# Sliding-window attention and a tanh layer on one core: which transposes go by DMA, which pairs stay uncast, and another list of steps

## The chip, the core and the metric

The kernel runs on one core of a Trainium2 chip. TensorE (PE) multiplies matrices and also transposes by a product with the identity; VectorE (DVE), ScalarE (ACT) and GpSimd (POOL) work on elements; SyncE (SP) only issues transfers here. POOL issues transfers too, those that change float32 to bfloat16 on the way. Each engine runs its own instructions in order and waits for others at semaphores. The metric is the device time of one execution in microseconds (us). The median of 3 runs of the kernel before is 319.51 us (318.67 to 321.03).

## The reference, cut to what matters

```python
batch, n_heads, seq, head_dim = (8, 8, 576, 64)          # q, k, v in float32
n_tokens, d_model, d_ff = (4608, 512, 2048)

def _attn_ref(q, k, v):
    scores = scale * np.matmul(q, k.transpose(0, 1, 3, 2))
    rel = pos[:, None] - pos[None, :]
    mask = (rel >= 0) & (rel < 64)
    scores = np.where(mask, scores, -1000000000.0)
    attn = softmax(scores)                               # exp, divided by its sum
    return np.matmul(attn, v)

def _moe_ref(x, w_in, w_out):
    h = x @ w_in
    g = h - np.tanh(h)
    return g @ w_out
```

x is the attention's result with the heads side by side: 4608 rows (8 batches of 576 positions) of 512. Each position sees itself and the 63 before it.

## The kernel before

**Tiling.** The eight heads of a batch are handled as four pairs (head r and head r + 4), so there are 32 pairs, pair g being of batch g // 4. The 576 positions are nine windows of 64; a window's queries meet 128 keys, its own 64 and the 64 before. The two layers behind the attention take the 4608 rows in nine chunks of 512 rows, eight windows each: chunk 2 holds windows 16 to 23, so six of its windows are batch 2's (18 to 26), and three of chunk 3's.

**Staging.** PE needs q, k and x with the feature on the partitions. Three ways lead there. (1) A pair's rows of q or k are loaded (words `lq`, `lk`), cast or laid side by side (`cq`, `ck`), transposed by PE in six products of 96 rows (`Ep` for q, `Fp` for k, line 261) and evicted from PSUM by ACT or DVE (`Ea`, `Eb`, `Ec`, `Fc`). A pair that is not cast is transposed straight from its loaded rows in 12 smaller products (line 257). (2) For k of batches 3 to 7, 128 positions at a time are loaded by POOL (`lr`) and transposed by DMA, issued on SP (`tk`, line 181). (3) For q of later batches a whole batch is loaded (`LQ`), spread by POOL into zeroed rows (`z`, then `cz`, line 128), written to device memory from SP (`bo`, line 133) and read back transposed, from SP again (`td`, line 138). In the kernel before, batches 6 and 7 take way 3. x is transposed either by PE (`Xp`, line 453) with evictions (`Xc`) or by DMA from SP (`Y`, line 472); in the kernel before batches 3 to 7 go by `Y`.

**The rest of a pair.** `Rp` makes the scores (lines 289, 294, 300), `Rx` the exponentials on ACT (line 305), `M` masks them on DVE, `LV`, `lv`, `lt` load V, `Z`, `za`, `zb` copy V's rows so that each window finds its 128 keys together (lines 166, 167). `P` and `PP` multiply by V (lines 405, 418), `D`, `DR`, `DN` divide by the sum (DVE). Batch 0's pairs mask by a product with `hide` ahead of the scores; the mask for the others, `seen`, is made by `n` and put into PSUM by `N`.

**The two layers.** For each chunk, 16 words `H` (four products each, line 489) make the first layer, `A` its tanh on ACT (line 497), `G` the difference on DVE (line 503); 16 words `W` (four products each, line 522) make the second layer and `O` evicts (ACT or DVE) and stores it from SP. w_in comes in three loads `wi`, w_out in four `wo`, on POOL.

**Order.** Nothing reorders at run time. A string PLAN holds one word per step, in the order in which the steps are issued; `play` goes through it. A word such as `Rp.12.0.4` is the scores of pair 12, group 0, in PSUM bank 4; a last letter names the engine (p POOL, a ACT, v DVE, s SP). Since each engine keeps its own order, a word's place says only what it stands behind on its own engine. `U` is a filler product on PE that nothing needs.

Of the kernel before, what the change touches and what calls it, by code (L numbers as in the profile page):

```python
# [9 lines left out]
ALU = mybir.AluOpType  # L10
# [5 lines left out]
def kernel(  # L16
# [21 lines left out]
    M = d_ff // 128  # L38
# [197 lines left out]

    def make_mask():
        nc.gpsimd.memset(seen, 1.0)
        nc.gpsimd.affine_select(seen, seen, compare_op=ALU.is_ge, fill=0.0,
                                base=-1, pattern=[[1, 128]], channel_multiplier=-1)  # L240
        nc.gpsimd.affine_select(seen, seen, compare_op=ALU.is_ge, fill=0.0,
                                base=64, pattern=[[-1, 128]], channel_multiplier=1)
# [241 lines left out]

    def hp_mm(c, m, s):
        n = columns(s)
        hp = ps[:, m % 2 if c > 1 or s is not None else m % 3, n]
        for ki in range(4):
            nc.tensor.matmul(hp, w_in_tile(ki, m),  # L489
                             chunk_tile(c)[:, n.start // 64:n.stop // 64, ki % 2, 64 * (ki // 2):64 * (ki // 2) + 64],  # L490
                             start=(ki == 0), stop=(ki == 3))
        return hp
# [70 lines left out]
    def subtract():  # L563
# [4 lines left out]
        i=make_ident, u=make_warm, mv=pads_v, mt=pads_k, mq=pads_q, mk=pads_kw, U=warm_up, h=make_hide, n=make_mask, N=put_mask,  # L568
# [15 lines left out]
        H=first_layer, A=tanh, G=subtract, W=lambda: yp_mm(*step("W")), O=lambda e: y_out(*step("O"), e))  # L584

    def play(script):
# [5 lines left out]
        lk.0.s lq.0.s u U.11 mq.0 mt.1 mv.0 lk.3.p i lk.1.p mt.0 cq.0.a ck.0.a Fp.0.2 Fc.0.2.a ck.1.a U.3  # L592
        Fp.1.2 lq.1.p cq.1.a mq.1 Ep.0.3 Ec.0.3.a Fc.1.2.v LV.0.3 LV.0.1 LV.0.4 LV.0.2 U.4 Ep.1.3 Ec.1.3.a h
        U.4 Rp.1.1.4 Rx.1.1.4 LV.0.0 Rp.1.0.0 lq.3.p lk.2.p Fp.3.2 Rx.1.0.0 Rp.0.1.4 Fc.3.2.a Rx.0.1.4
        Rp.0.0.0 mv.1 Z.0 lq.2.p U.2 Ep.3.3 Ec.3.3.a Rx.0.0.0 U.1 Fp.2.2 Rp.3.1.4 Ep.2.3 lk.4.p lk.5.p
        lk.7.p lq.5.p wi.0 lq.4.p n lq.7.p P.0 ck.5.v Fc.2.2.a Rx.3.1.4 Ec.2.3.a D.0 Rp.3.0.0 Fp.5.3
        Fc.5.3.v cq.5.v Rp.2.1.4 P.1 ck.4.a Rx.3.0.0 Ep.5.3 D.1 Rp.2.0.0 Ea.5.3.a Rx.2.1.4 Rx.2.0.0 wi.1
        lk.6.p wi.2 lq.6.p lv.1.0.1 lv.1.1.0 lv.1.0.0 lt.1 lv.1.1.1 P.3 Eb.5.3.v Rp.5.0.4 D.3 Fp.4.3
        Xp.0.0.1.2 Rx.5.0.4 Fc.4.3.a Xc.0.0.1.2.a P.2 Xp.0.0.0.3 N Rp.5.1.4 Xc.0.0.0.3.a Rx.5.1.4 D.2
        Xp.0.1.0.3 ck.7.v cq.4.v Xc.0.1.0.3.v Xp.0.1.1.2 Rp.5.2.4 Ep.4.3 Xc.0.1.1.2.a H H H Rx.5.2.4  # L600
        Ea.4.3.a A Eb.4.3.a A G A G G ck.6.v cq.7.v Rp.4.2.4 Fp.7.3 Rx.4.2.4 Fc.7.3.a H A Rp.4.0.4 Rx.4.0.4
        G H A G H Fp.6.3 A Rp.4.1.4 H H G Fc.6.3.a A A Rx.4.1.4 Ep.7.3 H M.5 G G A Ea.7.3.a cq.6.v G H H A A
        H A Eb.7.3.v Rp.7.2.4 Ep.6.3 Ea.6.3.a Rx.7.2.4 lq.8.p wo.0 lk.8.p lq.9.p wo.1 wo.2 zb.1.0.p za.1.1.p
        zb.1.1.p wo.3 lk.9.p lv.1.3.1 lv.1.3.0 lv.1.2.1 lv.1.2.0 G G G H H H A cq.8.v za.1.0.v G M.4
        Eb.6.3.a Rp.6.0.4 H Ep.8.3 A A Rx.6.0.4 A Rp.7.0.4 PP.4 Rx.7.0.4 Rp.6.2.4 G G G ck.8.v DR.4 DN.4.1
        DN.4.0 DN.4.2 Rx.6.2.4 cq.9.v W Rp.6.1.4 Ea.8.3.a Eb.8.3.a Rx.6.1.4 W W W Fp.8.3 Fc.8.3.v Rp.7.1.4 W
        Ep.9.3 Ea.9.3.v Rx.7.1.4 ck.9.v W W W O.a W Eb.9.3.a Fp.9.3 Rp.8.2.4 O.a M.6 lk.10.p lk.11.p
        lr.3.2.1 mk lr.3.2.0 lq.11.p W Fc.9.3.a Rx.8.2.4 Xp.1.0.0.3 W Rp.9.2.4 M.7 za.1.3.v zb.1.3.p
        zb.1.2.v za.1.2.v PP.6 DR.6 DN.6.2 DN.6.0 lq.10.p DN.6.1 Rx.9.2.4 Xc.1.0.0.3.a Rp.9.1.4 W Rx.9.1.4
        Xp.1.0.1.3 Xc.1.0.1.3.a Rp.8.0.4 W ck.10.v Rx.8.0.4 W Xp.1.1.1.3 Xc.1.1.1.3.a Rp.8.1.4 W LV.2.4  # L610
        LV.2.0 lr.3.0.0 LV.2.3 LV.2.2 lr.3.3.0 cq.10.v LV.2.1 lr.3.4.1 lr.3.0.1 lr.3.3.1 tk.3.3 tk.3.0
        tk.3.2 LQ.3 lr.3.1.1 lr.3.4.0 lr.3.1.0 Xp.1.1.0.3 W Rx.8.1.4 ck.11.v cq.11.v Xc.1.1.0.3.v Ep.10.3
        Ea.10.3.v Rp.9.0.4 tk.3.4 lr.4.2.0 tk.3.1 LQ.4 lr.4.3.0 LV.3.4 lr.4.1.0 lr.4.2.1 LV.3.3 lr.4.0.1
        lr.4.4.0 lr.4.0.0 lr.4.3.1 lr.5.0.1 tk.4.0 O.a O.a Eb.10.3.a H H A A H A Fp.10.3 M.8 G G H H G
        Rx.9.0.4 Fc.10.3.a A A Fp.11.3 Rp.10.1.4 H M.9 G G Fc.11.3.a Rx.10.1.4 A H A Rp.10.2.4 H Rx.10.2.4 A
# [74 lines left out]
```

## Time and profile before

| | |
|---|---|
| median of 3 runs | 319.51 us |
| the profiled execution's own time | 319.47 us |
| its span, from the first to the last instruction | 317.8 us |
| busy: PE, DVE, ACT, POOL | 305.3, 187.8, 173.2, 111.7 us |
| first-layer products (576) and second-layer products (560), mean of one | 379, 379 ns |
| first first-layer product | at 28.37 us |
| moved by DMA | 39.11 MB |
| fillers on PE | 25, 10.1 us busy |

A profile page shows the share of the span in which each engine was busy, the span in 40 slices with a digit of busy tenths each, the chain of work that ended last, and groups of instructions with their idle time and what released them. The timeline lists instructions by start and length. The weight loads of PE run beside its products, and a product's length overlaps the next one's. Idle time of an engine matters only where it sits on the chain.

### The profile page before, as it was taken

The numbers are of one execution on the slowest core, as the hardware profiler recorded it, in microseconds if no ns is written. First come the engines' busy times: TensorE is split into PE (matmuls) and PEld (weight loads), VectorE is DVE, ScalarE is ACT, GpSimd is POOL, SyncE is SP. The second block draws the span as 40 slices with busy tenths as digits, with TensorE's granted clock in tenths as the row PEclk, the third lists the DMA queues.
The fourth block names the chain that finished last, engine by engine and source line by source line (L and its number), as shares of the span: only waits on it lengthen the run. The fifth ranks groups of instructions, "written<-read, shape, count | busy, mean of one in ns | idle before, by whom it ended". The sixth has DMA issues, their size and how long they took to land.

```text
span 317.8 us, 6105 instructions
## 1 busy us (share of the span) xinstructions
PE 305.3 (96%) x2412; PEld 165.7 (52%) x2412; DVE 187.8 (59%) x321; ACT 173.2 (54%) x322; POOL 111.7 (35%) x164
## 2 busy tenths in 40 slices
PE   7878999999999999999799999999999999999995
PEld 2455565656655655555455555555554544445444
DVE  2355995489887896769374666566753554244400
ACT  4678885589778675555344635544524435334311
POOL 8982849985871384892021430000000000000000
PEclk9799999999999999999999999999999999999999
DMA  9999999999999699999998999262014010010021
GB/s 151 152 202 198 190 196 130 181 154 146 155 138 166 99 138 151 188 148 119 199 156 157 136 166 206 72 144 72 33 36 107 33 68 33 33 36 33 33 99 68
DMA packets 113133, 39.11 MB, mean 123 GB/s; under 512 B 96336, under 2 KB 107600, under 8 KB 113104
## 3 DMA queue, kind: packets, MB, share of 16 engines
q0 software_dynamic: 72064, 18.06, 66.4%
q1 hardware_dynamic: 41040, 20.65, 31.4%
q8 instruction: 19, 0.31, 0.4%
q14 instruction: 10, 0.08, 0.1%
HBM read 36.70 MB, written 11.80 MB: 153 GB/s over the span
## 4 chain that ended last, share of the span: by engine, by line
PE 86%; DMA 5%; DVE 4%; ACT 3%; issue 1%; SPq 0%; ACTq 0%; DVEq 0%
PE ps L489 37%; PE ps L522 36%; PE ps L300 4%; DMA xT<-xs 3%; PE ps L261 3%; PE ps L418 3%; PE ps L225 1%; DMA qf<-in_q_dram 1%; PE ps L516 1%; DVE xs L447 1%; PE ps L453 1%; ACT qt L88 1%; DVE qt L90 1%; DVE vw L167 1%; ACT pt L305 1%
## 5 line engine op out<-in xcount | busy, mean ns | idle before, releaser
L489 PE MATMUL ps<-xT,wi 128*128 128x512 bf16 x576 | 140.2, 379 | 2.4 <-DMA xT<-xs 1.7
L503 DVE TENSOR_TENSOR gT<-ps,th 128x512 bf16<-128x512 f32 x144 | 97.9, 689 | 72.5 <-ACT th L497 68.3
L522 PE MATMUL ps<-w_out_sb,gT 128*128 128x512 bf16 x560 | 135.9, 379 | 0.0
L497 ACT ACTIVATE th<-ps 128x512 f32<-128x512 f32 x144 | 85.3, 598 | 74.7 <-PE ps L489 70.9
L489 PEld LDWEIGHTS <-wi 128*128 128x128 bf16 x576 | 62.6, 113 | 53.6 <-DMA xT<-xs 1.8
L522 PEld LDWEIGHTS <-gT 128*128 128x128 bf16 x560 | 52.9, 98 | 55.3
L305 ACT ACTIVATE pt<-ps 128x384 bf16<-128x384 f32 (+1 forms) x92 | 46.0, 504 | 24.5 <-PE ps L300 23.0
L176 POOL DMA_DIRECT2D kall<-in_k_dram x50 | 37.2, 753 | 11.0 <-DMA vw<-in_v_dram 4.7
L160 POOL DMA_DIRECT2D vw<-in_v_dram x35 | 30.1, 866 | 12.3 <-PE ps L300 11.9
L88 ACT ACTIVATE ysb<-ps 128x512 f32<-128x512 f32 (+1 forms) x25 | 14.6, 582 | 29.4 <-PE ps L522 26.8
L393 DVE TENSOR_TENSOR pt<-pt,ps 128x1152 bf16<-128x1152 bf16 x28 | 20.7, 746 | 4.0 <-ACT pt L305 4.0
L128 POOL COPY qz<-qall 96x384 bf16<-96x384 bf16 x16 | 7.6, 517 | 41.4 <-DMA qd<-qz 35.7
L300 PEld LDWEIGHTS <-kw 128*128 128x128 bf16 x180 | 14.3, 98 | 10.9
L300 PE MATMUL ps<-qt,kw 128*128 128x128 bf16 x180 | 19.7, 219 | 0.0
L88 ACT ACTIVATE qt<-ps 64x576 bf16<-64x576 bf16 x25 | 16.1, 643 | 3.0 <-PE ps L300 1.5
L438 DVE TENSOR_TENSOR xs<-ps,rcp 128x384 bf16<-128x384 f32 x28 | 15.1, 552 | 0.3
L90 DVE COPY qt<-ps 64x576 bf16<-64x576 bf16 x15 | 11.3, 755 | 3.5 <-PE ps L261 2.0
L90 DVE COPY ysb<-ps 128x512 f32<-128x512 f32 x12 | 8.2, 685 | 7.9 <-PE ps L522 7.9
L418 PEld LDWEIGHTS <-pt 128*64 128x64 bf16 x504 | 9.2, 111 | 4.6 <-issue 2.4
L225 PE MATMUL ps<-warm 128*128 128x512 bf16 x25 | 10.1, 552 | 1.3 <-DVE warm L206 1.1
L418 PE MATMUL ps<-vw,pt 128*64 128x65 bf16 x504 | 10.7, 197 | 0.4 <-DVE vw L167 0.4
L261 PE MATMUL ps<-ident,qb 96*128 96x96 bf16 x132 | 9.6, 210 | 0.4 <-DVE qb L90 0.3
(68 smaller groups left out, 167.6 us busy)
## 6 DMA issues: line engine op xcount, KB each, us to landing
out_dram<-ysb SPq DMA_DIRECT2D x35, 256.0 KB, 2.3
vw<-in_v_dram POOLq DMA_DIRECT2D x28, 128.0 KB, 5.9
qall<-in_q_dram POOLq DMA_DIRECT2D x5, 576.0 KB, 8.9
kall<-in_k_dram POOLq DMA_DIRECT2D x40, 64.0 KB, 5.8
qd<-qz SPq DMA_DIRECT2D x8, 288.0 KB, 4.1
w_out_sb<-in_moe_w_out_dram POOLq DMA_DIRECT2D x4, 512.0 KB, 8.5
kall<-in_k_dram POOLq DMA_DIRECT2D x11, 144.0 KB, 5.1
qall<-in_q_dram POOLq DMA_DIRECT2D x11, 144.0 KB, 5.2
```

The costliest lines, as they stand in the source:

```text
L88: nc.scalar.activation(o, i, ACT.Copy)
L90: eng.tensor_copy(o, i)
L160: nc.gpsimd.dma_start(out=w[:, 2 * i + 1, :, 0:D] if i < NF else w[64:128, 2 * i, :, 0:D], in_=v[b, :, 128 * i:128 * i + n].rearrange("h p ...
L176: nc.gpsimd.dma_start(out=token_rows(b)[0:c, i, :, h, :], in_=k[b, NP * h:NP * h + NP, 128 * i:128 * i + c].rearrange("r p d -> p r d"))
L300: nc.tensor.matmul(sp[:, i], kt[:, 64 * j:64 * j + 128], qT[g % NR][:, :, 64 * j:64 * j + 64], start=first, stop=first or i == n - 1)
L305: nc.scalar.activation(PT[g % NPT][:, js[0]:js[0] + len(js), :].rearrange("p i (h t) -> p i h t", h=2), sp, ACT.Exp, scale=scale)
L393: nc.vector.tensor_tensor(p, p, mask.unsqueeze(1).to_broadcast([128, 2 * NJ, 64]), ALU.mult)
L418: nc.tensor.matmul(ps[r, bank, 65 * i:65 * i + 65], PT[(g + r2) % NPT][:, j, r], vw[b % 2][:, j, p0 + r2 + NP * h, :], start=True, stop=True)
L489: nc.tensor.matmul(hp, w_in_tile(ki, m), chunk_tile(c)[:, n.start // 64:n.stop // 64, ki % 2, 64 * (ki // 2):64 * (ki // 2) + 64], start=( ...
L497: nc.scalar.activation(th[:, n], hp, ACT.Tanh)
L503: nc.vector.tensor_tensor(gT[c][:, m, columns(s)], hp, th, ALU.subtract)
L522: nc.tensor.matmul(yp, gT[c][:, m, s * 128:(s + 1) * 128], w_out_sb[:, m, :], start=(m == 0), stop=(m == M - 1))
```

## The change

Five things differ.

1. q of batch 5 (pairs 20 to 23) takes way 3, over device memory, in place of PE; x of batch 2 goes by `Y` in place of `Xp` and `Xc`.
2. Pair 1 is no longer cast: pairs 1, 2 and 3 are now transposed uncast, pair 0 stays cast.
3. `seen` is made by one product of `hide` with the identity (`hn`) and one DVE operation, in place of three POOL operations.
4. The first three words of chunk 0's first layer are done in halves: `HA` takes the two products that need only x's first half (pairs 0 and 1 of the batch), the later `H` the other two.
5. PLAN is another list. Among the loads, q of pair 0 goes ahead of its k on SP, q of pair 5 comes second on POOL, V's rows come after some of q and k, and w_in and w_out come behind all of batch 1's q and k and some of batch 2's. Some evictions, casts and outputs change between ACT and DVE.

```diff
+    HALVED = 3
...
+    def turn_hide():
+        nc.tensor.matmul(ps[0:64, 6, 0:128], hide[:, 0], ident, start=True, stop=True)
+
     def make_mask():
-        nc.gpsimd.memset(seen, 1.0)
-        nc.gpsimd.affine_select(seen, seen, compare_op=ALU.is_ge, fill=0.0,
-                                base=-1, pattern=[[1, 128]], channel_multiplier=-1)
-        nc.gpsimd.affine_select(seen, seen, compare_op=ALU.is_ge, fill=0.0,
-                                base=64, pattern=[[-1, 128]], channel_multiplier=1)
+        nc.vector.tensor_scalar(seen, ps[0:64, 6, 0:128], 2.0 ** -30, 1.0, ALU.mult, ALU.add)
...
+    halved = {}
+
+    def half(c, m):
+        if c or m >= HALVED:
+            return slice(0, 4)
+        halved[m] = halved.get(m, 0) + 1
+        return slice(2 * halved[m] - 2, 2 * halved[m])
+
     def hp_mm(c, m, s):
         n = columns(s)
         hp = ps[:, m % 2 if c > 1 or s is not None else m % 3, n]
-        for ki in range(4):
+        for ki in (0, 2, 1, 3)[half(c, m)]:
...
-        H=first_layer, A=tanh, G=subtract, W=lambda: yp_mm(*step("W")), O=lambda e: y_out(*step("O"), e))
+        HA=lambda m: hp_mm(0, m, None), H=first_layer, A=tanh, G=subtract, W=lambda: yp_mm(*step("W")), O=lambda e: y_out(*step("O"), e))
...
     PLAN = """
-        lk.0.s lq.0.s u U.11 mq.0 mt.1 mv.0 lk.3.p i lk.1.p mt.0 cq.0.a ck.0.a Fp.0.2 Fc.0.2.a ck.1.a U.3
-        Fp.1.2 lq.1.p cq.1.a mq.1 Ep.0.3 Ec.0.3.a Fc.1.2.v LV.0.3 LV.0.1 LV.0.4 LV.0.2 U.4 Ep.1.3 Ec.1.3.a h
-        U.4 Rp.1.1.4 Rx.1.1.4 LV.0.0 Rp.1.0.0 lq.3.p lk.2.p Fp.3.2 Rx.1.0.0 Rp.0.1.4 Fc.3.2.a Rx.0.1.4
-        Rp.0.0.0 mv.1 Z.0 lq.2.p U.2 Ep.3.3 Ec.3.3.a Rx.0.0.0 U.1 Fp.2.2 Rp.3.1.4 Ep.2.3 lk.4.p lk.5.p
-        lk.7.p lq.5.p wi.0 lq.4.p n lq.7.p P.0 ck.5.v Fc.2.2.a Rx.3.1.4 Ec.2.3.a D.0 Rp.3.0.0 Fp.5.3
...
+        lq.0.s lk.0.s u U.8 mt.0 mq.1 mv.0 mt.1 i cq.0.a Ep.0.3 Ec.0.3.v mq.0 lq.1.p lq.5.p lk.1.p lq.3.p
+        lk.3.p ck.0.a U.1 Fp.0.2 Fc.0.2.a LV.0.0 lq.2.p LV.0.2 LV.0.3 h lk.2.p LV.0.4 LV.0.1 U.1 Ep.1.3
+        Ec.1.3.v U.2 Fp.1.2 Fc.1.2.a U.7 Rp.1.0.0 Rx.1.0.0 Rp.1.1.4 mv.1 Ep.3.3 Rp.0.0.0 Fp.3.2 Ec.3.3.v hn
+        Rx.1.1.4 n Rp.0.1.4 Fc.3.2.a Rx.0.1.4 Ep.2.3 N Ec.2.3.v cq.5.v U.1 Rp.3.1.4 Rx.0.0.0 Rp.3.0.0 Ep.5.3
+        Fp.2.2 Rx.3.1.4 Rx.3.0.0 Fc.2.2.a U.4 Rp.2.0.0 Ea.5.3.v Eb.5.3.a Z.0 U.1.5 P.0 lk.5.p ck.5.v Fp.5.3
+        Rp.2.1.4 D.0 lk.4.p lq.4.p lq.7.p lk.7.p lk.6.p lv.1.3.1 lq.8.p wi.0 lq.6.p wi.1 lk.9.p wi.2 lk.8.p
+        lv.1.1.1 lv.1.0.0 lt.1 P.1 ck.4.v D.1 Rx.2.0.0 Fc.5.3.a Rx.2.1.4 Fp.4.3 Rp.5.1.4 Fc.4.3.a Rx.5.1.4
+        Xp.0.0.0.3 P.2 Rp.5.0.4 Xc.0.0.0.3.a ck.7.v cq.4.v D.2 Rx.5.0.4 Ep.4.3 Xp.0.0.1.2 Xc.0.0.1.2.v P.3
+        Rp.5.2.4 Ea.4.3.a Eb.4.3.a Rx.5.2.4 Fp.7.3 Fc.7.3.a HA.0 Rp.4.1.4 Rx.4.1.4 D.3 Xp.0.1.1.2 Xp.0.1.0.3
+        HA.1 Rp.4.2.4 Xc.0.1.1.2.a ck.6.v cq.7.v Xc.0.1.0.3.v Rx.4.2.4 H H HA.2 A A Ep.7.3 H Rp.4.0.4
...
-        DN.8.1 Ep.13.3 Ea.13.3.a Rx.11.2.4 G G DN.8.2 M.11 H H H Eb.13.3.a A A A G G G Xp.2.0.1.3 PP.10
-        Rp.12.2.4 Xc.2.0.1.3.a Xp.2.0.0.3 Rx.12.2.4 W Rp.12.0.4 W Xc.2.0.0.3.a Rx.12.0.4 DR.10 DN.10.2
-        DN.10.1 DN.10.0 Xp.2.1.1.3 Rp.12.1.4 Rx.12.1.4 cq.14.v Xc.2.1.1.3.v W Rp.13.2.4 Xp.2.1.0.3 Rx.13.2.4
...
+        G DN.8.0 cq.13.v H H Rx.11.1.4 M.11 Eb.12.3.a A A A Ep.13.3 PP.10 G G DR.10 G DN.10.0 DN.10.2 H H
+        Ea.13.3.a Eb.13.3.a Rp.13.0.4 A cq.15.a A G H H Rx.13.0.4 DN.10.1 Rp.13.1.4 A A G G G H H H A
+        Rx.13.1.4 A A G G G Rp.12.0.4 Ep.15.3 Y.2 LV.3.3 LV.3.4 lr.5.4.0 LV.3.2 lr.4.4.1 lr.4.1.1 lr.5.3.1
+        lr.5.1.1 LV.4.1 lr.4.3.1 tk.4.0 tk.4.1 tk.4.4 tk.4.2 tk.4.3 LV.4.0 lr.5.0.0 LV.4.2 LV.4.3 Rx.12.0.4
+        Rp.12.1.4 Rx.12.1.4 cq.14.a LV.4.4 LQ.5 lr.5.3.0 lr.5.4.1 W Rp.13.2.4 W W W Z.3 Rx.13.2.4 Ea.15.3.a
+        Eb.15.3.a Rp.12.2.4 Rx.12.2.4 H Rp.15.0.4 Rx.15.0.4 O.v M.13 M.12 Ep.14.3 H Rp.15.2.4 W A A
...
+        W Rp.18.2.4 H A Rx.18.2.4 A Rp.19.0.4 W lr.6.2.1 lr.6.0.1 lr.6.1.1 lr.6.3.0 z cz.20 LV.5.4 lr.6.3.1
+        tk.5.2 tk.5.4 tk.5.1 bo.20 tk.5.3 lr.6.2.0 lr.6.4.0 cz.21 LV.5.3 Rx.19.0.4 bo.21 tk.5.0 O.a td.20
+        cz.22 cz.23 G G H A Rp.19.2.4 H A G G W H H W A A DN.16.2 DN.16.1 G G H Rx.19.2.4 A W M.18 G H A G W
+        Rp.19.1.4 Rx.19.1.4 M.19 H H td.21 O.a bo.22 W bo.23 A A DN.16.0 G W H G H A A PP.18 Rp.20.2.4
```

## The prediction

> **What bounds the kernel now.** I read the page's busy shares first, then the slices, then the chain that ended last.
>
> ```profile
> PE 305.3 (96%) x2412; PEld 165.7 (52%) x2412; DVE 187.8 (59%) x321; ACT 173.2 (54%) x322; POOL 111.7 (35%) x164
> ...
> PE   7878999999999999999799999999999999999995
> ...
> PEclk9799999999999999999999999999999999999999
> DMA  9999999999999699999998999262014010010021
> ...
> PE 86%; DMA 5%; DVE 4%; ACT 3%; issue 1%; SPq 0%; ACTq 0%; DVEq 0%
> ```
>
> TensorE (PE) is busy 96% of the span and carries 86% of the chain. So time can come from three places only: instructions taken off PE, PE's waits, and the stretch before the first layer starts, where PE is short of work. DMA is full until some 215 us, which matters for everything that is moved to it. I then took three stretches of the table by windows and the timeline.
>
> ```profile
> 0.00:28.50 28.50, 22.41 (x318) 12.69 (x319) 11.94 (x27) 17.89 (x30) 22.17 (x40) 0.94 1.43 176
> 28.50:45.00 16.50, 16.50 (x133) 9.75 (x132) 13.40 (x24) 15.22 (x31) 10.19 (x16) 1.00 1.36 195
> 150.00:160.00 10.00, 8.34 (x78) 4.50 (x77) 3.55 (x6) 3.87 (x8) 0.00 (x0) 1.00 1.40 178
> ```
>
> The columns are stretch, length, and busy time of PE, weight loads, DVE, ACT and POOL, then granted clock, DMA share, GB/s. Up to 28.5 us PE is idle for 6.1 us, and 10.1 us of its busy time is the 25 filler multiplies (word U). From 28.5 to 45 it has no gap. At 150 to 160 it loses 1.66 us, and the timeline says to what:
>
> ```profile
> 13.57 0.70 DVE L166 COPY vw<-vw 64x2080 bf16<-64x2080 bf16 x1 [2.66 <-DMA vw<-in_v_dram]
> ...
> 28.37 2.75 PE L489 MATMUL ps<-xT,wi 128*128 128x512 bf16 x12
> ...
> 31.12 0.56 POOL L197 DMA_DIRECT2D w_out_sb<-in_moe_w_out_dram  x1 [3.65 <-DMA wi<-in_moe_w_in_dram]
> ...
> 68.62 0.42 PE L261 MATMUL ps<-ident,kb 96*128 96x96 bf16 x6
> 68.88 0.33 PE L300 MATMUL ps<-qt,kt 128*128 128x128 bf16 x3
> ...
> 86.28 0.39 PE L453 MATMUL ps<-ident,xs 128*128 128x128 bf16 x4
> ...
> 86.50 1.03 PE L522 MATMUL ps<-w_out_sb,gT 128*128 128x512 bf16 x4
> ...
> 142.30 5.52 SPq L472 DMA_TRANSPOSE xT<-xs  x2
> ...
> 152.89 1.05 PE L489 MATMUL ps<-xT,wi 128*128 128x512 bf16 x4 [1.66 <-DMA xT<-xs]
> ```
>
> Since PE's durations overlap, an instruction's price is the time to the next start. Six transposes of q or k hold PE 0.26 us (68.62 to 68.88), four of x 0.22 (86.28 to 86.50), four of the large products 0.86.
>
> **Off PE in the steady part.** Batch 5's q goes by DMA: four Ep words of six transposes, 4 x 0.26 = 1.04 us. Batch 2's x goes by DMA: four Xp words, 18 transposes x 0.055 = 0.99 us. PE never waits there, so **2.0 us** come off the end. The evictions that go with them (eight of q, eight of x, some 0.4 to 0.75 us each on ACT or DVE) and four casts lie beside PE, where ACT is busy 15 of 20 us at most after 70 us: counted nothing; if ACT or DVE were late it would be a gain. Seven outputs moved from ACT (0.60 us) to DVE (0.68) are also hidden, as DVE is busy 59%.
>
> **On the start.** Pair 1 is no longer cast. ACT loses two casts of 0.83 us; PE transposes it in 24 instructions in place of 12, 0.38 against 0.27 us a word, +0.2. First batch evictions move from ACT to DVE, and the mask is made by one product and one DVE operation (no row; between the shortest PE interval, under 0.1 us, and the 0.3 us of a small DVE copy, hidden either way) in place of three POOL operations of 0.8 us. ACT had 17.89 of 28.5 us and sat in the path of pairs 0 to 3 (evictions and exponentials); DVE had 11.94. So the attention of the first four pairs can run earlier, until it meets V: the two V copies started at 13.57, when V had landed. In the new order 12 POOL loads (seven k or q, five V) end with V; the twelfth landing was 15.83 us in the trace, and the identity goes ahead of the loads on POOL (+0.5), so V is complete near 16.3, the copies (0.70 + 0.79) end near 17.9 and the first product with V starts at 18.0, against 18.28. No gain up to there. After it, the old order takes 1.8 to 2.4 us per pair (four reciprocals at 19.44, 21.46, 23.86, 26.00), since each waits for ACT's exponentials; with these done earlier I walk 19.3, 21.1, 23.1, 24.9. Halving the first three products (HA needs only pairs 0 and 1) lets PE begin them near 25.4. Walking on with the rows' durations, the first word H starts near 27.5, with 1.5 us more PE work behind it than at 28.37 in the old order (two halves of 0.43, Fp.7, two scores of 0.17). That would be 2.3 us; if the early clock is slower (below) some 0.8. I take **1.5**, bounds 0 and 2.3.
>
> The price is in the loads. POOL has at most eight loads out: w_out's first load is the eighth after w_in's last and was issued at 31.12, as that one landed (30.83). Five k, q or V loads now come ahead of w_in's first, 0.7 us each, so it lands near 25 (21.1 before), its last near 33.4 (30.8), and six of batch 2's loads ahead of w_out's last move that from 46.6 to about 50.7. First-layer products need w_in's last part near 34.5, second-layer ones w_out's third and fourth near 48 and 50.2. So 0 to 1.5 us of waits return; I take **0.7**.
>
> **On the SP queue.** Y.2 is issued when the last normalisation of batch 2 is done. From there to chunk 2's first product the new list has about 7 us of PE work (four large words W, three H, four scores, a transpose). Xc, the old way, needed one eviction. The ten x transposes of the trace landed in 2.3 to 12.7 us, those issued while loads ran (110 to 145 us) in 8.0 to 12.7. Behind it on SP wait batch 4's k transposes (tk.4), needed only some 16 us later. The stall is 0 to 3.7 us (7 against 10.5, the worst first landing); with POOL's loads landing in 4 to 6 us at this time of the old run I take **0.5**.
> Batch 5's q takes cz (POOL, 0.96 us) then bo and td on SP, each behind k transposes and outputs there. z (3.25 us) and cz stand on POOL ahead of batch 5's and 6's loads. I put bo.20 near 117 us and td.20 near 122, against a first use near 131. Bounces landed in 3.1 to 7.3 us, td in the same; 3 to 4 us are left over. Stall 0 to 4.4, taken **0.5**.
> Y.4, which cost 1.66 us, has 14 us of PE work between its batch's last normalisation and its first use, against 9 in the old list; its landing took 10.5. I take **-1.66**, bounds -1.66 and 0.
>
> **Sum**, against the profiled execution's own 319.47 us (span 317.8 and 1.7 around it; the runs' median is 319.51, the same): -2.0 + 0.2 - 1.5 + 0.7 + 0.5 + 0.5 - 1.66 = -3.3, so **316.1 us**. The tail of 3.5 us behind the last product is the same in both lists.
>
> A rule that speaks against the change: the Trainium skill ("VectorE: DVE Perf Modes", The three transpose paths) puts a 128x128 transpose at 390 ns on TensorE and 1309 ns by DMA, and advises TensorE. Taken as a series, an estimate from that page, Y.2's first twelve blocks would need 15.7 us, a stall of 8.7 and a time near 324. The trace does not agree: transfers of like size (eight to ten blocks) landed first in 2.3 to 10.5 us, and a block held PE only 0.055 us. What is left of the rule is the rival of late landings below, priced from rows alone.
>
> **Rivals.**
> *The start gives nothing* (chance 0.25). The clock was 0.50 between 10 and 12 us and a filler took 0.43 us, not 0.22, after a stretch of PE idle from 5.9 to 9.2. The new list has seven fillers near 8.5 to 10 us; at the slow clock they end at 11.5, and the chain to the first product shifts by 1.5 us. Together with 1 us of late weights the gain of 0.8 is gone: 316.1 + 0.8 + 1 = about 318. For it: the early idle is there in the new list too, waiting for k of pair 1 near 8.1. Against: more transposes lie in that stretch.
> The Trainium skill ("TensorE: Matmul & The Clock Gate", Part 1: The HAM clock gate) says the clock is halved by windows of 3.4 us that run free of the kernel; the slow stretch of 9.2 to 12.6 us agrees, so the phase may differ from run to run.
> *Late landings* (0.2), the slower side. Transposes behind a full load queue land as Y.3 and Y.4 did. At 10.5 us Y.2 stalls PE 3.7; at 6.6 for bo.20 and 11.8 for td.20, its scores stall 4.4. That is 8.1 in place of the 1.0 in the sum: 323.2. It decides from a landing of 7 us for Y.2, and of 14 for bo and td together. For it: the DMA row is 9 throughout. Against: SP's transfers at 81 to 88 us landed in 3.2 to 4.3.
> *All fits* (0.1): 2.3 at the start, no new stalls, 319.47 - 2.0 + 0.2 - 2.3 - 1.66 = about 313.7.
> The forecast keeps 0.45. That the transposes do not leave PE is excluded by the list itself.
>
> **Numbers.** One per cent (3.2 us) is about what measurement tells from no change: below 316.3 is faster, above 322.7 slower. Faster: half of the forecast's 0.45, all of the last 0.1, a little of the first rival, 0.08: 0.40. Slower: 0.6 of late landings and the tail of the rest, 0.17. Same: 0.43. The forecast alone spans 314 to 318; with the rivals 313 to 322.5.
>
> **What would show it.** In the changed profile: 24 fewer transposes of q and 18 fewer of x on PE; the first product with V near 18; the first layer's products (halves) from about 25.4, whole words from 27.5; PE's waits for xT below 1 us at Y.2 and gone at Y.4; PE's waits for w_in or w_out together below 1.5 us; no wait of a score for qt near 131. Wrong it would be if PE waits for xT near 85 us for more than 3 us, if fillers near 9 us take 0.43 us, or if ACT or DVE becomes what the products wait for in chunks 1 and 2.

## The result, and the profile after

The changed kernel takes **333.07 us** (median of 4 runs, 327.90 to 335.91), the kernel before beside it 320.27 (318.67 to 322.09). The ratio is **1.0292, 95% interval 1.0222 to 1.0362**: slower by some 3%. The forecast was 316.1, with a range up to 322.5. The profiled execution of the changed kernel is one of its longest (335.91 us, span 334.0), so the waits below are at their upper size (19.5 us in all with what follows them, where the ratio stands for a loss of 9.3), and the ratio leaves such executions out.

The page of the changed kernel: busy time, three rows of the 40 slices, and the engines' shares of the chain that ended last.

```profile
PE 310.6 (93%) x2383; PEld 166.1 (50%) x2383; DVE 182.9 (55%) x315; ACT 165.8 (50%) x306; POOL 115.1 (34%) x172
...
PE   7879999999769999995999949999999999999995
...
PEclk9989999999969999999799997999999999999999
DMA  8999999999999999999998999165004001100022
...
PE 68%; DMA 19%; POOL 5%; DVE 3%; issue 2%; ACT 1%; DVEq 0%; POOLq 0%; ACTq 0%
```

PE's share of the chain fell from 86% to 68%, DMA's rose from 5 to 19%. The PE row has holes in slices 11 and 12, 19 and 24 that the row before had not, and the PEclk row dips in slice 12 and in 20 and 25, just behind each, and in slice 3, in the opening. PE is longer busy although the list gives it less to do, mostly because a product at half the clock takes twice as long.

The table by windows of the changed kernel (stretch, length, busy PE, weight loads, DVE, ACT, POOL, granted clock, DMA share, GB/s), the first two stretches being those of the prediction:

```profile
0.00:28.50 28.50, 23.36 (x341) 13.91 (x342) 14.91 (x34) 16.52 (x26) 22.74 (x39) 0.94 1.34 168
28.50:45.00 16.50, 16.50 (x142) 9.74 (x141) 14.13 (x26) 14.78 (x30) 8.94 (x14) 1.00 1.54 173
86.00:100.00 14.00, 8.91 (x45) 4.06 (x43) 6.09 (x9) 5.29 (x11) 12.05 (x17) 0.81 2.58 138
150.00:163.00 13.00, 8.73 (x40) 4.05 (x39) 5.51 (x9) 3.84 (x8) 1.26 (x2) 0.87 1.58 205
192.00:204.00 12.00, 7.80 (x34) 3.35 (x33) 5.36 (x8) 3.15 (x6) 0.84 (x2) 0.86 1.96 173
```

The same view of the kernel before has 14.00, 11.34 and 12.00 us of PE busy in the last three, at a clock of 1.00. What PE waited for there, from the timeline of the changed kernel (start, length, instruction, in brackets the idle time ahead of it and what ended it):

```profile
18.84 0.51 PE L405 MATMUL ps<-vw,pt 128*64 128x65 bf16 x20 [0.29 <-DVE vw L168]
22.96 0.35 PE L300 MATMUL ps<-qt,kt 128*128 128x128 bf16 x3 [1.50 <-ACT pt L305]
27.33 0.60 PE L497 MATMUL ps<-xT,wi 128*128 128x512 bf16 x2
...
91.64 0.96 DVE L167 COPY vw<-vw 64x2080 bf16<-64x2080 bf16 x1 [7.80 <-DMA vw<-in_v_dram]
94.36 1.46 PE L530 MATMUL ps<-w_out_sb,gT 128*128 128x512 bf16 x4 [4.36 <-DVE ysb L91]
96.55 1.87 PE L497 MATMUL ps<-xT,wi 128*128 128x512 bf16 x4 [0.73 <-DVE gT L511]
...
142.86 5.24 SPq L472 DMA_TRANSPOSE xT<-xs  x2
148.88 2.58 SPq L139 DMA_TRANSPOSE qt<-qd  x1
158.92 0.34 PE L300 MATMUL ps<-qt,kw 128*128 128x128 bf16 x3 [4.27 <-DMA qt<-qd]
159.10 3.07 PE L530 MATMUL ps<-w_out_sb,gT 128*128 128x512 bf16 x8
...
182.97 5.48 SPq L472 DMA_TRANSPOSE xT<-xs  x2
188.55 3.52 SPq L139 DMA_TRANSPOSE qt<-qd  x1
...
193.58 0.70 DVE L167 COPY vw<-vw 64x2080 bf16<-64x2080 bf16 x1 [2.45 <-DMA vw<-in_v_dram]
...
200.18 0.51 PE L300 MATMUL ps<-qt,kw 128*128 128x128 bf16 x6 [3.39 <-DMA qt<-qd]
200.52 3.52 PE L530 MATMUL ps<-w_out_sb,gT 128*128 128x512 bf16 x8
```

(Line numbers moved by the edit: 497 is the first layer, 530 the second, 139 the word `td`, 167 and 168 the copies of V.) Three places:

- **At 90 us, V of batch 3.** The word `Z.3` copies V's rows on DVE. It waited 7.80 us for a load of V. Behind it on DVE stood `O.v`, which empties the PSUM bank that PE's next second-layer product writes; so PE, which needed no V yet, stood 4.36 us.
- **At 154 us, q of pair 22** (`td.22`). It was issued on SP at 148.88, behind the 5.24 us of `Y.4`, and landed at 158.88, 10.0 us later. On the other queue the 576 KB load of batch 7's q was out from 145.08 to 155.73.
- **At 196 us, q of pair 27** (`td.27`), behind `Y.5`: issued at 188.55, landed at 200.13. The shorter wait just ahead, at 195, is another one: on DVE `Z.6` waited 2.45 us for V of batch 6, and PE then stood 0.81 us for gT, which DVE made behind it.

Behind each wait come products at half the clock: eight of them take 3.07 us at 159.10 and four 1.87 at 96.55, where eight take 1.89 elsewhere (at 152.76 in the same timeline). Measured from start to start against the usual step, the waits are 4.5 + 1.15, 4.4, and 1.0 + 3.55 us, together 14.6, and the slow products 1.9 + 1.5 + 1.5, together 4.9. **335.9 - 14.6 - 4.9 = 316.4**: without these three places the changed kernel would be where the sum of the prediction put it. That it is so near 316.1 is partly luck: the sum had a gain of 0.6 us at the start and 1.0 us of stalls for `Y.2` and `td.20`, and neither came.

How the load came so late is told by the chain of the changed kernel (start, length, what):

```profile
60.97 8.68 DMA qall<-in_q_dram
69.95 14.51 DMA kall<-in_k_dram
84.75 6.82 DMA vw<-in_v_dram
```

A load of q (576 KB) lets a load of k go, which takes 14.51 us for 64 KB, and this one lets the last load of V go. V of batch 3 was complete at 91.6 us, and in the kernel before at 89.5, so it is only 2.1 us later. But the list asks for it earlier. In the kernel before, DVE did `Z.3` at 96.81, without a wait:

```profile
96.81 0.70 DVE L166 COPY vw<-vw 64x2080 bf16<-64x2080 bf16 x1
```

Now it came to this word at 83.84 (91.64 less the 7.80 it waited), 13 us earlier, and the first scores of batch 3 started at 77.5 us against 82.2. By the PE work of the words ahead of them, added up, `Z.3` stands some 11.5 us earlier in the new list and these scores 4.5. Of POOL's 128 loads 70 had landed by 90 us, before 79. The transposes moved to DMA added 2.93 MB (39.11 to 42.04).

### The profile page after: what moved, and what is told of

The parts are those of the page before. It is cut to its first block, busy times and chain, and to the rows that moved or that the text cites. A ratio compares the mean times of both kernels' runs of the same rounds, so it can differ in the third digit from the quotient of the medians.

```text
span 334.0 us, 6047 instructions
## 1 busy us (share of the span) xinstructions
PE 310.6 (93%) x2383; PEld 166.1 (50%) x2383; DVE 182.9 (55%) x315; ACT 165.8 (50%) x306; POOL 115.1 (34%) x172
## 2 busy tenths in 40 slices
DMA packets 121068, 42.04 MB, mean 126 GB/s; under 512 B 103504, under 2 KB 115536, under 8 KB 121040
## 4 chain that ended last, share of the span: by engine, by line
PE 68%; DMA 19%; POOL 5%; DVE 3%; issue 2%; ACT 1%; DVEq 0%; POOLq 0%; ACTq 0%
PE ps L530 30%; PE ps L497 30%; DMA qt<-qd 6%; DMA vw<-in_v_dram 5%; DMA kall<-in_k_dram 4%; DMA qall<-in_q_dram 4%; PE ps L300 3%; PE ps L418 2%; POOL vw L161 1%; POOL kall L177 1%; PE ps L524 1%; POOL qall L109 1%; DVE gT L511 1%; POOL kall L109 1%; PE ps L261 1%
## 5 line engine op out<-in xcount | busy, mean ns | idle before, releaser
L497 PE MATMUL ps<-xT,wi 128*128 128x512 bf16 x576 | 142.2, 384 | 1.8 <-DVE gT L511 1.5
L530 PE MATMUL ps<-w_out_sb,gT 128*128 128x512 bf16 x560 | 138.5, 386 | 4.7 <-DVE ysb L91 4.4
L305 ACT ACTIVATE pt<-ps 128x384 bf16<-128x384 f32 (+2 forms) x92 | 45.5, 503 | 44.8 <-PE ps L300 39.2
L129 POOL COPY qz<-qall 96x384 bf16<-96x384 bf16 x24 | 11.5, 522 | 45.6 <-DMA qd<-qz 45.5
L300 PEld LDWEIGHTS <-kw 128*128 128x128 bf16 x180 | 14.6, 101 | 21.4 <-DMA qt<-qd 8.6
L91 DVE COPY ysb<-ps 128x512 f32<-128x512 f32 (+1 forms) x19 | 12.8, 673 | 17.8 <-PE ps L530 16.7
L89 ACT ACTIVATE ysb<-ps 128x512 f32<-128x512 f32 (+1 forms) x18 | 10.5, 586 | 22.8 <-PE ps L524 16.8
L89 ACT ACTIVATE qt<-ps 64x576 bf16<-64x576 bf16 x27 | 17.3, 642 | 3.2 <-PE ps L261 2.3
L167 DVE COPY vw<-vw 64x2080 bf16<-64x2080 bf16 x7 | 5.3, 761 | 10.6 <-DMA vw<-in_v_dram 10.2
L226 PE MATMUL ps<-warm 128*128 128x512 bf16 x25 | 8.7, 472 | 1.0 <-DVE warm L207 1.0
L300 PE MATMUL ps<-qt,kt 128*128 128x128 bf16 x72 | 8.1, 223 | 1.5 <-ACT pt L305 1.5
```

Of the source, the lines that this page charges most:

```text
L89: nc.scalar.activation(o, i, ACT.Copy)
L300: nc.tensor.matmul(sp[:, i], kt[:, 64 * j:64 * j + 128], qT[g % NR][:, :, 64 * j:64 * j + 64], start=first, stop=first or i == n - 1)
L305: nc.scalar.activation(PT[g % NPT][:, js[0]:js[0] + len(js), :].rearrange("p i (h t) -> p i h t", h=2), sp, ACT.Exp, scale=scale)
L497: nc.tensor.matmul(hp, w_in_tile(ki, m), chunk_tile(c)[:, n.start // 64:n.stop // 64, ki % 2, 64 * (ki // 2):64 * (ki // 2) + 64], start=( ...
L530: nc.tensor.matmul(yp, gT[c][:, m, s * 128:(s + 1) * 128], w_out_sb[:, m, :], start=(m == 0), stop=(m == M - 1))
```

## The experiments

Theory from this profile: the list takes the second batches' attention ahead of what DMA can bring, and what is asked for too early or too late then stops PE. Rivals: one wrong place (the word `Z.3`, the transposes by DMA themselves) or the new start. Each ratio is to the kernel before, run beside it on the same chip.

**Z.3 later.** Only this word moves, to just ahead of the product that needs V.

```diff
-  W Rp.13.2.4 W W W Z.3 Rx.13.2.4
+  W Rp.13.2.4 W W W Rx.13.2.4
...
-  G H A G G PP.12
+  G H A G G Z.3 PP.12
```

> The V copies of batch 3 (word Z.3) are moved on DVE from ahead of the output O to just ahead of PP.12, nothing else. In the changed kernel's profile PE stood still for 0.8 + 4.5 + 1.2 us around 83 to 96 us and then ran 3.4 us at half clock (1.9 us more), while DVE waited 7.8 us for V in front of an output that PE's bank waited for. Theory A (the order on DVE puts a wait for late V in front of work that PE needs): the wait at 90 us is gone and 5 to 8 us come off, so some 323 against 329.5 for the changed kernel; at PP.12 at most 1 us comes back. Rival B (V itself is late because DMA has more to carry, and PE must wait for it wherever the copies stand): the wait moves to PP.12 and under 3 us come off, 327 or more.

Measured: 332.0 us, ratio 1.0389 (1.0329 to 1.0449). Waits of PE in this kernel (total, times, longest):

```profile
PE ps L300 <- DMA qt<-qd: 6.7, 2, 4.2
PE ps L418 <- DVE vw L168: 3.3, 1, 3.3
```

The wait moved to the product itself. The place of `Z.3` on DVE is not the cause; V is late.

**Batch 5's q by PE again, batch 2's x by PE again, and all three.** `cz`, `bo`, `td` of pairs 20 to 23 become `cq`, `Ep`, `Ea`, `Eb` at the same places; `Y.2` becomes four `Xp`, `Xc`, and `Ep.15` comes a few words later.

```diff
-  lr.6.3.0 z cz.20
+  lr.6.3.0 z cq.20.a
...
-  O.a td.20
+  O.a Ep.20.3 Ea.20.3.a Eb.20.3.v
...
-  Rp.12.0.4 Ep.15.3 Y.2
+  Xp.2.0.1.3 Xc.2.0.1.3.a Rp.12.0.4 Xp.2.0.0.3
```

> The q of batch 5 goes through PE again (four casts, four Ep with their evictions) where the changed list had td.20 to td.23; the bounces bo.20 to bo.23 are gone, Y.2 and everything else stay. Theory A (each DMA-fed word waits where its own slack is too short): the wait for qt at 154 us (4.4, and 1.5 of half clock behind it) goes, 1.0 us of PE work comes back, the waits at 90 us and at 196 us stay: 4 to 5 us faster than the changed kernel, some 325. Rival B (added DMA traffic makes all landings late): the wait at 196 us for td.27 goes too, 10 us faster, some 319.5. Rival C (the loads of batch 6 and 7 hold the queues, not the bounces): a wait for something else takes its place and under 2 us come off.

> The x of batch 2 goes through PE again (four Xp, four Xc) in place of Y.2; everything else as in the changed list. The V of batch 3 that DVE waited for landed at 91.6 us, 4 us after Y.2's first and 1.2 us after its second transfer. Theory A (V is late by its place in POOL's list and by the eight loads ahead of it): V lands at most 1 us earlier, 1.0 us of PE work comes back, the time stays within 1.5 us of the changed kernel. Rival B (Y.2's two transposes delay V): V lands 3 us earlier or more, the wait at 90 us shrinks to under 1.5 us, 3 to 6 us come off, 324 to 327.

> All three together: V copies late, batch 5's q and batch 2's x on PE; left of the change are the new start, pair 1 uncast, the halves and the rest of the list. Theory A: 8 off at 90 us, 5 at 154 us, 1 back, the wait for td.27 near 196 us (6 us with its half clock) stays or shrinks: 318 to 322 against 320 before. Rival B (volume): all three waits go, 314 to 317. If the start of the new list costs by itself, the time stays above 323, and the first first-layer product of a full word or chunk 1 starts later than before (28.4 and 64.1 us).

Measured: q on PE 340.31 us, 1.0634 (1.0568 to 1.07); x on PE 328.46, 1.0288 (1.0212 to 1.0364); all three 336.81, 1.042 (1.0333 to 1.0507). Putting q back took the wait at 154 away, but at the places where I put them the steps made waits of their own (3.0 us for gT at 128, 1.4 at 144), and k of batch 3 was late in that profile (3.3 us at 78). So it says what this list does with q on PE, not what q by DMA costs. x on PE is clearer: 75 loads had landed by 90 us against 70, V was there at 89.1, and between the opening and 149 us no wait above 1.1 us was left; yet the time hardly moved, since 3.6 us for td.22 at 149 and 2.1 (behind V of batch 6) + 1.1 (td.27) at 190 stayed. With all three, DMA moved 39.11 MB, as in the kernel before, and td.27 still took 12.0 us to land and cost a wait of 6.0, so the transposes that the change added are not what makes it late. `Y.2` itself landed in 9.4 us without a wait for xT; its price was paid by V's loads.

**Grafts.** The new list up to its first word `W` and then what is left of the old one; and the reverse. Steps that the one part has behind the seam and the other ahead of it were put at the seam. The first graft there:

```diff
   PP.4 Rx.7.1.4 Rp.7.2.4 Fc.8.3.a Rx.7.2.4
-  W Fp.9.3 Rp.7.0.4 W W M.6 DR.4 DN.4.1 Rx.7.0.4
+  Rp.7.0.4 Rx.7.0.4 DR.4 DN.4.1 DN.4.0 DN.4.2 cq.9.v W W W W W Ep.9.3
```

> The new list up to the first word of the second layer (start, pair 1 uncast, halves, mask, order of the first loads), then the old list: x of batch 2 and q of batch 5 go through PE as before. Words that only the one side had stand at the seam. Theory A (the loss lies in the rest, whose attention runs ahead of its loads): equal to the kernel before within 1.5%, 317 to 322. Rival B (the start costs, its loads reach w_out and V later and the delay never comes back): 324 or more.

> The old list up to the first word of the second layer, then the new list with x of batch 2 and q of batch 5 by DMA. Theory A: 7 us or more slower than before, 327 to 333, with PE waits near 85 to 95 us for what V of batch 3 holds up and near 150 and 195 us for qt. Rival B (the start costs): within 1.5% of before.

Measured: new start 324.6 us, 1.0149 (1.0096 to 1.0203); new rest 328.62, 1.0289 (1.025 to 1.0327). The rest has the waits for qt again, 4.1 us for td.22 at 151 and 1.6 at 192 in the profile, but not the one for V, which had landed at 89.2; and some 5 us of its waits lie at the seam, at 46 to 52, so its ratio is no clean measure. Nor is that of the start. In its profile the timeline of DVE, POOL and PE shows:

```profile
112.27 4.57 DVE L91 COPY qb<-qall 96x768 bf16<-96x768 bf16 x1
113.85 2.76 POOL L236 MEMSET qz<- 96x1536 bf16 x2
118.14 3.12 PE L497 MATMUL ps<-xT,wi 128*128 128x512 bf16 x7 [2.42 <-DVE gT L511]
```

A cast of q that takes 0.35 us elsewhere took 4.57 and ended just behind the zeros (word `z`) that POOL wrote; PE lost 2.4 us and then 1.5 at half clock. The cast had started 1.58 us ahead of the zeros, while POOL issued loads.

**The zeros moved**, in the graft with the new start.

```diff
-  LV.4.4 lr.5.1.1 tk.5.1 LQ.5
+  LV.4.4 lr.5.1.1 tk.5.1 z LQ.5
...
-  LQ.6 lr.5.4.1 z lr.6.0.1
+  LQ.6 lr.5.4.1 lr.6.0.1
```

> The new start with the old list behind it, as in the run before, and one word moved: the zeros of qz (two memsets on POOL) from 113.9 us to ahead of batch 5's q load, near 86 us, where DVE copies only out of PSUM. In the profile of that run the zeros stood from 113.85 to 117.3 us minus a load, and DVE's cast of q, 0.35 us elsewhere, took 4.57 us and ended 0.26 us behind them; PE then waited 2.4 us for gT and ran 1.5 us at half clock. Theory (the zeros hold the cast): cast back at 0.35 us, no wait for gT, 320 to 321 and a ratio of 1.000 to 1.005: the new start by itself gains and costs nothing. Rival (the new start costs the 1.5 %): 323 to 325, ratio 1.010 or more.

Measured: 322.17 us, 1.0062 (1.0023 to 1.01). The wait at 115 is gone, and over half of the loss with it. But the zeros met another cast, from the timeline of DVE and POOL:

```profile
85.05 2.79 DVE L91 COPY qb<-qall 96x768 bf16<-96x768 bf16 x1
84.82 2.80 POOL L236 MEMSET qz<- 96x1536 bf16 x2
```

That cast again ends with them, and cost PE 1.55 us. So the mechanism stands and my choice of a quiet place was wrong. The 2.0 us that are left of the loss are, but for 0.4, this wait: the new start by itself neither gains nor costs what can be told.

**Less to load.** The loads of q of batches 4 to 7 (2.36 MB) are left out.

```diff
-        nc.gpsimd.dma_start(out=t, in_=(q if n == "q" else k)[b].rearrange("h (p e) d -> p h (e d)", e=E))
+        if b < 4:
+          nc.gpsimd.dma_start(out=t, in_=(q if n == "q" else k)[b].rearrange("h (p e) d -> p h (e d)", e=E))
```

> The changed kernel without the four loads of q of batches 4 to 7 (576 KB each as stored): the casts and bounces read what stood in the tile, so the output is not the reference's; every instruction of PE, DVE, ACT and SP is there. The load of batch 4's q took some 5 us of the transfers right ahead of V of batch 3, those of batches 6 and 7 stand ahead of td.22 and td.27. Theory A (the DMA supply is the second bound): the waits at 90, 154 and 196 us shrink together, 9 to 18 us faster than the changed kernel, 312 to 321. Rival B (waits of a fixed latency, whatever else is in flight; or an order on a queue): under 4 us come off, 325 or more.

Measured: 321.75 us, 1.0103 (1.0043 to 1.0163), that is two thirds of the loss gone with the list untouched. V of batch 3 was there at 83.0 us and its wait was gone; one of the two waits for qt stayed, now for pair 27 (3.63 us at 185), with half clock behind it. Behind `Y.4` as before, td.22 landed in 6.3 us and nobody waited for it; behind `Y.5` td.27 still took 9.7. So at 154 us it is the load of batch 7's q that made the transpose late, more than its place behind `Y.4`.

**V first.** The four later loads of batch 3's V move up on POOL, right behind the first.

```diff
-  tk.3.4 LV.3.1 lr.4.3.0 lr.4.2.1 LQ.4 LV.3.0 lr.4.1.0
+  tk.3.4 LV.3.1 LV.3.0 LV.3.3 LV.3.4 LV.3.2 lr.4.3.0 lr.4.2.1 LQ.4 lr.4.1.0
...
-  Y.2 LV.3.3 LV.3.4 lr.5.4.0 LV.3.2 lr.4.4.1
+  Y.2 lr.5.4.0 lr.4.4.1
```

> Only the order of loads on POOL: the four other loads of batch 3's V go right behind the first, ahead of batch 4's q and most of its k. Theory A with order as the cause: V of batch 3 has landed by 82 us, Z.3 and the output behind it don't wait, 6 to 8 us come off (322 to 325); k or q of batch 4 may be 2 us late. Rival (supply as the cause, order cannot help): the wait returns as one for batch 4's k or q or for V of batch 4, and under 3 us come off.

Measured: 329.46 us, 1.0286 (1.023 to 1.0343). V landed by 77.4, `Z.3` ran at 83.7 without a wait, and PE stood 4.7 us at 146 and 3.2 at 188 for td.22 and td.27. One of three places removed, and the time is the same. So an earlier issue does bring V earlier, by 14 us, though DMA is full; batch 4's q, now behind it, landed 2.5 us later.

**The two transposes ahead.** `td.22` could not simply be moved ahead of `Y.4`: q by DMA had two buffers, and pair 20's last scores, which read td.22's buffer, stand behind `Y.4`. So pairs from 20 on rotate through three. The kernel has V first as well.

```diff
-    qT = [const.tile([128, 2, S], BF16, name=f"qt{i}") for i in range(NR)]
+    qT = [const.tile([128, 2, S], BF16, name=f"qt{i}") for i in range(3)]
...
-        nc.sync.dma_start(out=qT[g % NR].rearrange("c h s -> c (h s)"),
+        nc.sync.dma_start(out=qT[g % NR if g < 20 else g % 3].rearrange("c h s -> c (h s)"),
...
-  H W Y.4 O.v
+  H W td.22 Y.4 O.v
...
-  A Rx.20.0.4 G td.22 lr.7.3.1
+  A Rx.20.0.4 G lr.7.3.1
...
-  LV.6.4 bo.26 cz.28
+  LV.6.4 bo.26 bo.27 cz.28
...
-  G bo.27 O.a
+  G O.a
...
-  Y.5 LV.7.1
+  td.27 Y.5 LV.7.1
...
-  G td.27 O.a
+  G O.a
```

> The changed kernel with batch 3's V loads in the order of the run before (all behind the first of them) and two transposes of q taken out from behind the attention rows' ones: td.22 ahead of Y.4, td.27 ahead of Y.5 with its bounce behind that of pair 26. So that they may be issued there at all, q by DMA rotates through three buffers instead of two. The profile of the run with V first had two long waits left, 4.7 us at 146 and 3.2 us at 188, both for qt, each with half-clock products behind it (1.5 and 1.4 us), 10.8 us in all, at an own time of 326.9. Theory (order: the list asks for these two transposes too late, behind 5 us of SP and 9 us of other transposes): both waits under 1 us, 317 to 321. Rival (supply: the DMA engines are full until 190 us, whatever is put ahead makes something else late): a wait of 2 us or more for xT, or for k or V, at a later place, 324 to 329.

Measured: 322.34 us (10 runs, 317.76 to 327.25), **1.0025 (0.9974 to 1.0077)**. By this ratio the loss is gone within the error; the median of the ten runs is still 0.9% above that of the kernel before (319.46). From 1.0286 to 1.0025 is 8.4 us of 320, near the 10.8 that the two waits and their half clock had come to in the profile of V first. td.22 was now issued at 140.85, ahead of the load of batch 7's q (145.88), and landed in 3.3 us; td.27 took 8.4 us (8.3 to 12.0 in the profiles where it stands behind `Y.5`), but it was issued at 178.38 in place of 188.55. Yet the rival was half right: in this profile a new wait stands at 104, from its timeline:

```profile
109.05 0.48 PE L300 MATMUL ps<-qt,kw 128*128 128x128 bf16 x3 [4.64 <-DMA kw<-kall]
```

The last transpose of batch 4's k was issued at 98.04, 0.56 us behind a 576 KB load of q on the other queue; they landed together, at 108.9 and 109.0. The Trainium skill ("DMA: Bandwidth & Descriptors", Queues, rings and completion order) says that the queues of different issuers lie on the same 16 engines, each of which goes round among them packet by packet. That the two landed together agrees with shared engines; in which turns they work no run here shows.

**That load later, and the transposes ahead without V first.** The first is the kernel just told with one word moved, five loads later in POOL's order; the second is it without the edit of V's loads.

```diff
-  LV.4.4 LQ.5 lr.5.3.0 lr.5.4.1
+  LV.4.4 lr.5.3.0 lr.5.4.1
...
-  lr.5.0.1 lr.6.4.1 lr.5.1.0 LV.5.2
+  lr.5.0.1 lr.6.4.1 lr.5.1.0 LQ.5 LV.5.2
```

> The kernel of the last run of the changed list (V first, td.22 and td.27 ahead, three buffers) with one load moved: batch 5's q (576 KB) from ahead of the last transposes of batch 4's k to three loads later. In the profile of that run the last k transpose was issued at 98.04 us, half a microsecond behind this load, both landed together at 108.9 and 109.0, and PE stood 4.6 us for it at 104, with 2 us of half clock behind. Theory (order of the loads, the list is slower only by what it asks for too late): the transpose lands by 104, the wait is under 1 us, 317 to 320, ratio 0.990 to 1.002. Rival (supply): q of batch 5 or the loads behind it hold something else at 105 to 135 us for 2 us or more, 321 to 325, ratio 1.003 to 1.015.

> The changed kernel with the two transposes of q ahead and the third buffer, but with batch 3's V loads where the change has them. Theory (two independent late things): the V wait of 4.5 us at 90 stays with its half clock, 6 to 7 us, and the waits for qt at 154 and 196 go below 1.5 us: 322 to 326, ratio 1.008 to 1.02, so that V first by itself is worth as much behind this edit as is missing to 1.0025. Rival (the waits replace one another: a PE held at 90 gives the loads time): one of the later waits is gone without this edit being its cause, or V first adds nothing, ratio within 0.005 of 1.0025.

Measured: q later 326.73 us (6 runs), 1.012 (1.0056 to 1.0183). The k transpose landed at 104.5, in 6.4 us, and its wait fell to 0.2. But two loads of q were now out between 104 and 120, both of them from 106 to 114; `Y.3`, issued at 109.22, landed at 122.17, and PE waited elsewhere (timeline, then waits):

```profile
122.21 1.05 PE L497 MATMUL ps<-xT,wi 128*128 128x512 bf16 x4 [1.50 <-DMA xT<-xs]
```

```profile
PE ps L300 <- DMA qt<-qd: 6.7, 3, 4.4
PE ps L497 <- DMA xT<-xs: 4.0, 3, 1.5
```

Here the rival, supply, is right: one load out of the way puts another in it. Batch 7's q, too, was now loaded 5 us earlier than in the run before (140.87), beside td.22, which was issued at 140.67, ahead of `Y.4`, and yet landed only at 152.83, 12.2 us later. The transposes ahead without V first: 324.03 us, 4 runs from 318.10 to 330.59, too far apart for an interval. In its profile the waits for qt were 1.1 us and less, and the one for V at 91 was there (3.0, with half clock), as the theory had it; by how much V first adds stays open.

**Both relieved.** V first, the two transposes ahead, and q of batches 4 to 7 not loaded: the three edits shown above in one kernel.

> The kernel with V first, td.22 and td.27 ahead and three buffers, and in it the loads of q of batches 4 to 7 left out (2.36 MB of the 18.06 MB that POOL's queue moves; what is computed from q of these batches is then from what lies in the buffers, so the outputs of batches 4 to 7 aren't the reference's). Theory (two causes and no third: q's two transposes asked for too late, and loads that don't come faster than before while the list wants them earlier): the wait of 4.8 us for k at 104 and the ones for qt go, no wait over 1.5 us is left behind 60 us, and the time is what the prediction's own sum had without its added waits, 314 to 317, ratio 0.98 to 0.995: the saved PE work shows. Rival (something else in the list costs, in the tail or in the clock): 318 or more, ratio 0.997 or more, without such waits.

Measured: 316.66 us (315.64 to 317.31), **0.9882 (0.9828 to 0.9936)**, inside what the theory gave. The longest waits of PE in this kernel:

```profile
PE ps L301 <- ACT pt L306: 2.1, 2, 1.5
PE ps L301 <- DMA kw<-kall: 1.0, 1, 1.0
```

The first is in the opening, as in every kernel with the new start. With the two transposes asked for earlier, V's loads first and 2.36 MB less to load, no long wait and no loss are left, so a further cause of any size is not there. How the loss divides among the three stays open. It is no proof that the saved PE work alone makes the 1.2%, as loads are missing too.

**x by PE and the two transposes ahead**, two edits shown above, and a kernel that computes everything:

> The changed kernel with td.22 and td.27 ahead and three buffers, V's loads where the change has them, and batch 2's rows turned by TensorE as before (18 products more, two transposes on the DMA queues less). With that part alone V of batch 3 came in time (75 loads landed by 90 us against 70, no wait over 1.1 us before 149), and 9.3 us were left in its profile: 3.6 and 2.5 of half clock at 149, 2.1 and 1.1 at 190, at an own time of 328.4. Theory: these go with the two transposes ahead, 318 to 321, ratio 0.995 to 1.005. Rival (supply: other waits come in their place, as with q of batch 5 moved): a new wait of 2 us or more between 90 and 160, 322 to 327, ratio 1.007 to 1.025.

Measured: 327.78 us, 4 runs from 322.62 to 330.94, no interval. In the profile of the 322.62 the waits for td.22 and td.27 were gone and one of 3.3 us for qt stood at 152: td.23, issued at 145.95 behind `Y.4`, landed at 155.46. The rival again. No version that computes everything beat the kernel before; the one with V first and the transposes ahead cannot be told from it by its ratio.

## Why the prediction was wrong, step by step

- **Off PE, -2.0, and Y.4's wait, -1.66: held as far as can be seen.** There is no wait for xT at `Y.4`, neither in the changed kernel, where PE had already waited for td.22, nor with both causes relieved (landed at 142.9, first used at 150.2); without the three places 316.4 us are left, and 316.66 were measured with both causes relieved. Neither was measured by itself.
- **The start, -1.5 + 0.7 + 0.2: next to nothing came.** V was complete at 17.3 us (16.3 predicted), the first product with V came at 18.84 (18.0), the halves at 27.33 (25.4). The walk of 1.8 us from pair to pair failed at the third, where PE waited 1.50 us for ACT's exponentials at 22.96: the casts went from ACT, but the exponentials still pace the pairs. The second chunk's first product came at 65.14 against 64.05, with 1.2 us more PE work done ahead of it, a gain of 0.1; in the graft it came at 64.15, with only 0.2 us more work ahead of it, again a gain of 0.1. The last load of w_in landed at 35.0 (33.4 predicted) and that of w_out at 53.3 (50.7), yet the waits for weights were 0.4 us. So the rival *the start gives nothing* had the outcome right, but not by its slow fillers: from 8 to 13 us the clock was 1.00. Nor had PE been idle from 5.9 to 9.2 in the kernel before, as that rival has it: it waited there twice, 0.86 and 0.82 us, and worked between. It was 0.50 from 23.1 to 26.5 us instead, behind the wait of 1.50. The halves came 8.5 us behind the first product with V there, and 7.8 in the six profiles with the same start that had no half clock in it.
- **Y.2, +0.5: right for xT, wrong for the rest.** It landed in 9.4 us, and chunk 2's first product did not wait, with 0.2 us to spare, since PE took 9.5 us to get there and not the 7 of the sum. The step priced the transposes by their own landing; what they delayed was V (V at 91.6 with `Y.2`, at 89.1 without).
- **td.20, +0.5: the right mechanism at the wrong pair.** td.20 and td.21 landed in 4.0 and 4.6 us and nobody waited. td.22 and td.27 stood behind `Y.4` and `Y.5` and took 10.0 and 11.6. The rival *late landings* names this, and its 323.2 are too low because it walked `Y.2` and td.20 alone. In the profile the two waits and their half clock are 11.0 us, where the sum has 0.5. The step should have walked every `td` against what is out beside it, the `Y` on SP and the 576 KB loads on POOL, and asked from when its buffer is free.
- **The step that failed: "which matters for everything that is moved to it".** I saw that DMA is full until 215 us and then priced only the transposes that the change moved to it. The list also moved the demand: batch 3's scores some 4.5 us and `Z.3` 11.5 us of PE work earlier, with V of batch 3 there 2.1 us later than before. The sum has no term for a load behind the opening, and the stretch at 90 us, 7.5 us in the profiled execution, is not in it in any form.
- **Half clock.** The prediction spoke of it for the start alone. Behind the three places it made 4.9 of the 19.5 us lost.

## What to carry to other kernels

When a list of steps is moved forward on one engine, walk each load and transfer that it needs from its issue to its landing in the old trace, against its new place; with a full DMA row a load that is asked for earlier lands earlier, but something else lands later. Price a short transfer by what is out beside it, on its own queue and on the others, not by its size, and ask for it early; a buffer count can be what keeps it from going ahead. In these traces a wait of 3 us on TensorE cost more than 3 us: price the slow products behind it.

## What the runs showed of the hardware that was not expected

- **Half clock after short waits.** Behind 60 us all 20 waits of 2.8 to 6.0 us in these profiles were followed by a stretch of half clock, as was one of 2.42 us (seven products in 3.12 us); one of 2.53 and those of 1.0 to 1.9 were not. Each stretch was 3.41 or 6.83 us long; a large product took 0.427 us in it in place of 0.216, so seven of them cost 1.5 us more. The Trainium skill ("TensorE: Matmul & The Clock Gate", Part 1: The HAM clock gate) names an idle window of about 3.4 us; the 2.42 us wait is shorter, and four large products ran right ahead of it. The length of the wait does not decide alone: behind the 1.50 us wait of the opening the clock (the figure behind POOL's) was halved in the changed kernel

```profile
24.00:28.50 4.50, 4.50 (x78) 3.77 (x78) 3.17 (x8) 3.74 (x7) 1.49 (x3) 0.72 1.22 197
```

  and not in the graft with the same opening and the same wait:

```profile
24.00:28.50 4.50, 4.18 (x74) 3.16 (x68) 3.67 (x10) 4.27 (x10) 2.31 (x4) 1.00 1.21 209
```

- **POOL's zeros hold a DVE cast.** Twice a cast of 0.35 us ended with POOL's two memsets, after 4.57 and 2.79 us; in the kernel before a copy of V beside the same zeros took 1.86 us (at 115.81) in place of 0.70. Meanwhile DVE operations that read PSUM ran beside the zeros at their usual length (0.73 us at 117.81 in the changed kernel). What held the first cast for the 1.58 us ahead of the zeros is not shown. The Trainium skill ("SBUF — State Buffer", Who interferes with whom) has it that the port pair DVE shares with GpSimd is an exclusive lock; the two pairs of rows agree for the time of the zeros.
- **Landing times grow with what else is out.** Batch 5's transposes of q at 133 to 136 us landed in 4.0 and 4.6 us. td.22 landed in 9.8 to 12.2 us in the six profiles where the load of batch 7's q was already out or went out with it, and in 3.0 to 6.3 in the five where that load came later or was left out, whether it stood behind `Y.4` or ahead of it. td.27 took 8.3 to 12.0 us behind `Y.5` and 8.2 to 10.3 ahead of it, and 3.5 in the kernel before, issued at 167.8. A 64 KB load of k took 14.5 us at 70 us.
